# Packed attention and a two-layer MLP on one Trainium2 core: the same steps in another written order

## The chip, the core and the metric

The kernel runs on one core of a Trainium2 chip. A core has five engines that run side by side and wait for each other by semaphores: TensorE (PE in the profile; its weight loads are a row of their own, PEld), VectorE (DVE), ScalarE (ACT), GpSimd (POOL) and SyncE (SP). Matrix products go to PSUM, eight banks of 128 partitions by 512 fp32 values, and VectorE or ScalarE copy them out to SBUF. Transfers are issued from GpSimd (here the loads, which also turn fp32 into bf16) and from SyncE (here the stores and the crossbar transposes), and run on 16 DMA engines that all share. The metric is the time of one execution on the device, in microseconds (us). Each execution is timed apart; one more is taken with the hardware profiler.

## The reference

Eight batches b, eight heads, 576 positions, head size 64, and 32 packed queries p per head; then an MLP over all 4608 positions.

```python
def sm_attn(qq, kk, vv):
    s = scale * qq @ kk.T
    a = exp(s - max(s))
    return (a / (sum(a) + 1e-09)) @ vv
p_packed = sm_attn(p, k, v)              # 32 rows per head
x = sm_attn(q, p_packed, p_packed)       # 576 rows per head; heads side by side: 4608 x 512
r = maximum(x @ w_in, 0)                 # 512 -> 2048
out = (s * r * r + b) @ w_out            # 2048 -> 512, fp32
```

## The kernel before

The order of all work is written out by hand: a list of words (lines 686 to 763), run one after the other by `run` (line 638). The first engine to reach an instruction whose inputs aren't ready waits; each engine keeps its own order. A word names a step, a batch and a part; `@n` gives the PSUM banks that the step takes; a final `a` or `v` says whether ScalarE or VectorE does the step's copy; a word that comes again takes the step's next stage. The words:

- `Lk`, `Lq`, `Lv`, `Lp` load k, q, v, p of a batch (lines 124 to 153; batch 0 in parts), `Lwi6.8` loads columns 1536 to 2047 of W_in (256 per unit, line 161), `Lwo` four blocks of W_out (line 167), `Lpall` p of batches 2 to 7, `Lsb` s and b. All of these are issued by GpSimd, in the order of the words. There is one buffer each for raw k, q and v, so a load waits until the batch before has been read. GpSimd runs ahead of the words where its waits let it; it may have eight loads out.
- `PD`, `PP`, `PA`, `PPA` double p and transpose it on TensorE.
- `Tk`, `Tq` (line 222, and 248 for q of batch 0) transpose k and q of batches 0 and 1 on TensorE, with copies out of PSUM. From batch 2 on `Dk`, `Dq` (line 261) have the DMA crossbar do it: one instruction on SyncE for each, which waits for its own load and for the last reader of the destination. kT and qT have two buffers each. SyncE runs in order, so a transpose that waits also holds the stores behind it.
- `F` (line 280) is the first scores of p against k, with exp on ScalarE; `V` (line 268) reorders v on VectorE; `P` (line 305) is the packed sum over v, its reciprocal and scaling; `X` (line 332) transposes the result.
- `S` (line 339; for batch 0 in parts of 384 and 192 columns, line 366) is the second scores and exp. The sums, their ln and exp(-ln) are `A` (line 434), for batch 0 the words `d`, `l`, `i`, `G`. The weights are not applied to packed values first: `W` (line 449; 415 for batch 0) multiplies the packed values by W_in, and `M` (line 501; `h`, line 473, for batch 0) multiplies that by the attention weights, so that a hidden block of 128 rows comes out transposed, is put through relu by ScalarE or VectorE, and squared by VectorE into gT.
- `O` (line 549) does some of the 16 accumulating matmuls of a tile of 128 output rows with W_out; `Q` (line 566) scales and adds the bias while copying out on VectorE, and stores. `BT` (line 515) sums W_out for that bias.
- `Z` (line 596) is matmuls on zeros whose result nobody reads[...].

O1.4 is tile 4, counted from 0, of batch 1; A1.0 is head set 0 of batch 1; M1.8 is hidden block 8 of batch 1; a name like Q0.3 or F5.0 is read likewise. Batches overlap: while the M and O words of one batch fill TensorE, F, P, X, S, A and W of the next are spread in between. Twelve Z stand ahead of the list (line 684).

In the profile all matmuls have line 62, transposes on TensorE line 65, and all instructions of the other engines line 73, since helpers record them; groups are told apart by their tiles: kn, qn, vn are raw k, q, v, kT and qT their transposes, pw the W results, rlu the relu, ysb an output tile, banks PSUM, zb the zeros.

Of the kernel before, what the change touches and what calls it, by code (L numbers as in the profile page):

```python
# [14 lines left out]
def kernel(  # L15
# [670 lines left out]
    for word in """  # L686
        Lq0.1 PD0 PP0@1 PP0v Z4@0 Tk0.0@2 Tk0.0v Z2@0 Tk0.1@4 Tk0.1v Tk0.1v PP0a Tk0.0a F0.0@6 V0.0 F0.0
        F0.1@0 F0.1 Lp1 Z2@3 P0.0@2 P0.0 V0.1 Z3@6 X0.0 X0.0a Z1@0 P0.1 P0.1 Z3@0 X0.1 X0.1a Tq0.0@4
        Tq0.0a Z1@2 Tq0.1@3 S0.0.0@6 Tq0.1a Tq0.0v Tq0.1v S0.0.1 e0.0 e0.1 Lk1 Z1@2 S0.1.0@0 S0.1.1 e1.0
        Z1@3 d0.0@4 Lwi6.8 PD1 PP1@2 PP1v d0.1 e1.1 d1.0@6 Lwi2.4 l0.0 l0.1 d1.1 Z4@3 Tk1.1@0 l1.1 PP1v  # L690
        Tk1.1v i0.0 Tk1.0@2 Tk1.0v Tk1.0v Lwi0.1 i0.1 l1.0 i1.0 Tk1.1a Z1@6 F1.0@4 Lv1 F1.1@6 G0.1 G1.0
        Lq1 G0.0 i1.1 W0.7@0 W0.7v W0.6@2 W0.7a h0.14.0@0 h0.14.0v W0.6a W0.6a h0.12.0@2 G1.1 F1.1
        Lwi1.2 Lwi4.6 h0.14.0 Z1@6 W0.2@6 W0.2v W0.3@0 F1.0 h0.14.1@4 W0.2v h0.12.0a h0.12.0 W0.3v W0.3v
        h0.4.1@2 h0.4.1a h0.4.0@6 W0.0@2 W0.0v W0.0a h0.4.1 h0.6.1@0 h0.14.1v h0.6.1a h0.6.1 V1 h0.6.0@2
        h0.12.1@0 h0.14.1 h0.0.0@4 h0.4.0a h0.12.1a h0.4.0 h0.0.1@6 h0.0.1a h0.0.1 h0.0.0a P1.1@0 P1.1
        Z5@1 X1 h0.6.0a X1a h0.12.1 h0.0.0 Tq1.0@6 Tq1.0a Tq1.0a Tq1.1@4 W0.1@2 W1.3@0 Tq1.1v Tq1.1v
        S1@6,4 Lwo0.4 W0.1v W0.1a h0.2.0@2 W1.3v S1 W1.3v Lpall S1 h0.2.1@6 h0.2.1a A1.0@0 A1.0 W0.5@4
# [12 lines left out]
        M1.11@0 M1.11a W2.2a W2.2v O1.2x4@4 O1.0x2 O1.4x1 M1.11 M1.13 M2.14@0 M2.14a M2.15@2 O1.2x1  # L710
        O1.1x1@5 M2.15a M2.5@0 M2.15 O1.2x2 M2.5a M2.5 M2.0@2 M2.0a M2.4@0 O1.1x3 Lv3 M2.14 M2.10@2
        M2.4a PPA0 M2.10a M2.0 M1.15@0 M1.15v M1.15 O1.1x1 O1.0x1 O1.1x1 M2.6@2 O1.4x1 M2.8@0 M2.10
        M2.6v Dk4 M2.8a M2.8 O1.1x4 O1.2x1 M2.3@2 M2.3a O1.4x1 O1.2x3 O1.4x1 M2.1@0 O1.1x1 M2.3 Lk3 M2.4
        M2.1a M2.1 M2.12@2 M2.12a O1.1x2 O1.4x1 O1.2x1 O1.0x1 Dk3 O1.1x1 O1.0x3 M2.11@0 M2.11a M2.2@2
        M2.6 O1.2x1 M2.2v M2.11 O1.4x2 O1.2x1 M2.7@0 M2.7a V3 O2.0x1@2 O1.3x4@3 O1.1x1 O1.3x2 O1.0x1
        Q1.0 Lv4 O1.4x2 O1.2x1 Q1.4 O1.2x1 M2.2 Q1.2 Dq3 M2.12 M2.13@0 O1.1x1 Lq4 O2.0x4 O1.3x2 M2.13v
        O1.3x1 M2.7 O1.3x3 M2.9@6 PPA0 O1.3x4 Q1.3 M2.9a M2.9 Q1.1 O2.0x1 PPA0 M2.13 F3.0@0 F3.0 F3.1@6
        O2.0x4 F3.1 O2.0x1 O2.1x1@3 P3.1@4 P3.1 O2.0x2 V4 O2.0x3 Q2.0 X3 X3a O2.1x3 S3@0,6 S3 S3 W3.1@4
        W3.1v O2.2x1@2 W3.1v O2.2x2 A3.0@0 O2.2x1 A3.0 A3.0 A3.0 O2.1x1 A3.1@6 A3.1 A3.1 O2.2x5 Lv5
        W3.3@4 W3.3v W3.3a A3.1 W3.0@0 W3.0a W3.2@6 O2.2x5 W3.2a O2.2x1 O2.1x1 W3.2v W3.0v M3.5@4 M3.5a  # L720
        M3.10@6 M3.2@0 M3.2a M3.10v M3.5 M3.11@4 O2.2x1 M3.11a M3.1@6 M3.10 M3.12@0 M3.2 M3.1a M3.13@4
# [71 lines left out]
```

## Time and profile before

| | |
|---|---|
| median of 3 executions | 250.98 us (249.93 to 251.01) |
| the profiled execution, its own time | 249.54 us |
| its span | 247.8 us |
| busy: TensorE, VectorE, ScalarE, GpSimd | 235.5, 160.7, 125.6, 31.8 us |
| granted TensorE clock | 1.0 throughout |
| DMA, mean over the span | 143 GB/s, 35.53 MB |
| loads by GpSimd's queue | 18.58 MB |
| transposes and stores by SyncE's queue | 16.55 MB |

The span runs from the first to the last instruction of the profile, and the execution's own time holds what lies around it too. "Busy" of TensorE holds matmuls whose ends are modelled, so that 95% is not 95% of what it could do. "Waited for" lists name the engine or transfer whose semaphore came last ahead of a start. In a row of stretches, a DMA share of 1.00 is all 16 engines busy by the packets' own times; it can exceed 1, as packets overlap.

### The profile page before, as it was taken

What the parts mean: (1) busy time and instruction counts of PE and PEld (TensorE: products, weight loads), DVE (VectorE), ACT (ScalarE), POOL (GpSimd) and SP (SyncE); (2) the same over time, 40 slices, a digit from 0 to 9 for tenths busy, and PEclk for the clock granted to TensorE, in tenths of its full rate; (3) what the DMA queues carried; (4) which work ended last, traced back from release to release, by engine and by line L of the source; (5) the groups of instructions that cost most, each with busy time, mean ns of one, the idle gap of its engine ahead of it and who ended that gap; (6) DMA issues with size and microseconds to landing.
All of it is one profiled execution on the core that took longest, in us unless ns stands there. A gap on an engine that the chain in (4) does not pass through costs nothing.

```text
span 247.8 us, 5628 instructions
## 1 busy us (share of the span) xinstructions
PE 235.5 (95%) x2299; PEld 133.9 (54%) x2333; DVE 160.7 (65%) x326; ACT 125.6 (51%) x223; POOL 31.8 (13%) x45
## 2 busy tenths in 40 slices
PE   8998999998999998999999999999999999999993
PEld 2564655554556544476446645574547554675442
DVE  4438999978786477688279815983478725981232
ACT  2477798142874314865258704991288415880000
POOL 8563322001201010300110200102000000000000
PEclk9999999999999999999999999999999999999999
DMA  6999999999996889898839598998758040200135
GB/s 97 182 201 203 203 196 207 184 156 208 185 220 105 144 133 273 166 206 139 163 56 230 114 190 166 170 162 116 169 101 174 0 108 22 74 14 24 52 75 148
DMA packets 60522, 35.53 MB, mean 143 GB/s; under 512 B 32720, under 2 KB 56016, under 8 KB 60496
## 3 DMA queue, kind: packets, MB, share of 16 engines
q0 software_dynamic: 26272, 18.58, 52.8%
q1 hardware_dynamic: 34176, 16.55, 30.3%
q8 instruction: 18, 0.29, 0.5%
q14 instruction: 8, 0.07, 0.1%
q10 hardware_dynamic: 48, 0.03, 0.0%
HBM read 37.23 MB, written 9.44 MB: 188 GB/s over the span
## 4 chain that ended last, share of the span: by engine, by line
PE 82%; DVE 8%; ACT 3%; DMA 3%; issue 3%; DVEq 0%; ACTq 0%
PE banks L62 80%; DMA qT<-qn 3%; PE banks L65 2%; DVE ysb L73 2%; DVE rlu L73 2%; DVE gT L73 1%; DVE aT L73 1%; ACT rlu L73 1%; DVE pbd L73 1%; DVE kT L73 1%; ACT e L73 1%; DVE pw L73 1%; ACT rcd L73 1%; ACT pw L73 0%; ACT ld L73 0%
## 5 line engine op out<-in xcount | busy, mean ns | idle before, releaser
L62 PE MATMUL banks<-w_out_sb,gT 128*128 128x512 bf16 (+1 forms) x562 | 135.2, 373 | 2.7 <-issue 1.3
L62 PEld LDWEIGHTS <-gT 128*128 128x128 bf16 x592 | 55.9, 98 | 55.1 <-issue 4.3
L73 ACT ACTIVATE rlu<-banks 128x576 bf16<-128x576 f32 (+2 forms) x102 | 60.8, 656 | 36.1 <-PE banks L62 32.8
L62 PE MATMUL banks<-aT,pw 128*128 128x288 bf16 (+2 forms) x512 | 74.0, 286 | 2.2 <-DVE pw L73 0.9
L62 PEld LDWEIGHTS <-pw 128*128 128x128 bf16 x512 | 48.9, 98 | 25.2 <-issue 3.0
L73 DVE TENSOR_TENSOR gT<-rlu 128x576 bf16<-128x576 bf16 (+2 forms) x128 | 56.0, 455 | 9.9 <-ACT rlu L73 5.5
L73 DVE SCALAR_TENSOR_TENSOR ysb<-banks,svec,biasrep 128x512 f32<-128x512 f32 (+1 forms) x37 | 26.7, 733 | 37.5 <-PE banks L62 37.3
L73 ACT ACTIVATE e<-banks 96x768 bf16<-96x768 f32 (+3 forms) x34 | 21.8, 694 | 41.6 <-PE banks L62 41.6
L73 DVE CAST pw<-banks 128x512 bf16<-128x512 f32 (+1 forms) x40 | 23.5, 618 | 6.6 <-PE banks L62 6.6
L73 DVE TENSOR_SCALAR rlu<-banks 128x576 bf16<-128x576 f32 (+2 forms) x26 | 19.6, 761 | 6.0 <-PE banks L62 5.1
L73 POOL DMA_DIRECT2D qn<-in_q_dram x9 | 6.9, 773 | 81.1 <-DMA qT<-qn 77.5
L73 ACT CAST pw<-banks 128x512 bf16<-128x512 f32 (+1 forms) x32 | 15.8, 556 | 1.9 <-PE banks L62 1.9
L62 PE MATMUL banks<-zb 128*128 128x512 bf16 x37 | 12.7, 463 | 1.6 <-DVE zb L73 1.2
L73 DVE TENSOR_TENSOR aT<-e,rcd 128x576 bf16<-128x576 bf16 (+2 forms) x18 | 11.8, 685 | 1.6 <-ACT rcd L73 1.6
L62 PE MATMUL banks<-w_in_sb,ppd 64*32 64x512 bf16 (+1 forms) x288 | 11.2, 357 | 0.1
L73 POOL DMA_DIRECT2D kn<-in_k_dram x9 | 7.2, 805 | 29.7 <-DMA kT<-kn 23.9
L73 ACT ACTIVATE rcd<-ld 128x576 f32<-128x576 f32 (+2 forms) x18 | 10.8, 631 | 0.2
L62 PEld LDWEIGHTS <-ppd 64*32 64x32 bf16 x432 | 5.3, 89 | 10.1 <-issue 6.4
L73 ACT ACTIVATE ld<-banks 128x576 f32<-128x576 f32 (+2 forms) x18 | 10.2, 594 | 0.9 <-PE banks L62 0.4
L73 POOL DMA_DIRECT2D vn<-in_v_dram x9 | 7.0, 782 | 17.5 <-DVE vr L73 16.9
L73 DVE COPY vr<-vn 96x3072 bf16<-96x3072 bf16 (+1 forms) x9 | 7.8, 862 | 1.8 <-DMA vn<-in_v_dram 1.8
L73 DVE RECIPROCAL rd<-banks 128x2 f32<-128x2 f32 (+1 forms) x9 | 1.5, 169 | 10.6 <-PE banks L62 10.6
(54 smaller groups left out, 100.0 us busy)
## 6 DMA issues: line engine op xcount, KB each, us to landing
out_dram<-ysb SPq DMA_DIRECT2D x23, 192.0 KB, 3.4
kn<-in_k_dram POOLq DMA_DIRECT2D x7, 576.0 KB, 8.5
vn<-in_v_dram POOLq DMA_DIRECT2D x7, 576.0 KB, 9.3
qn<-in_q_dram POOLq DMA_DIRECT2D x7, 576.0 KB, 7.2
out_dram<-ysb SPq DMA_DIRECT2D x24, 128.0 KB, 2.6
w_out_sb<-in_moe_w_out_dram POOLq DMA_DIRECT2D x4, 512.0 KB, 18.1
w_in_sb<-in_moe_w_in_dram POOLq DMA_DIRECT2D x3, 512.0 KB, 11.5
out_dram<-ysb SPq DMA_DIRECT2D x23, 64.0 KB, 2.6
```

What stands on the lines that cost most here:

```text
L62: return tc.keep_in_program_order(nc.tensor.matmul(*a, **kw))
L65: return tc.keep_in_program_order(nc.tensor.transpose(*a, **kw))
L73: return lambda *a, **kw: tc.keep_in_program_order(f(*a, **kw))
```

## The change

Only the list of words changes, and with it the order of instructions on each engine. The multiset of TensorE's steps is the same but for Z: 41 matmuls on zeros before, 42 after. What moves:

- At the start, the transposes of k of batch 0 stand ahead of p's. The second scores of batch 0 are done for 192 columns first, then for 384. Four W words, not two, precede the first `h`.
- GpSimd's loads behind q of batch 0 were: p1, k1, W_in 1536-2047, 512-1023, 0-255, v1, q1, W_in 256-511, 1024-1535, W_out, pall, the rest of W_out, s and b, k2, q2, v2, q3, k4, v3, k3. They become: W_in 0-255, p1, W_in 1536-2047, 256-511, 512-1023, k1, v1, q1, W_in 1024-1535, W_out, s and b, pall, the rest of W_out, q2, k2, v2, v3, q3, k3, k4.
- `Tk1` and `F1` move from ahead of the hidden blocks of batch 0 into them.
- SyncE's order was: kT2, qT2, stores, kT4, kT3, stores, qT3, and so on. It becomes: kT2, the store of O0.3, qT2, stores of batch 0, kT3, qT3, stores, kT4, and so on. Later transposes move too.
- Some copies and relus go from ScalarE to VectorE or back: relus of `h` were 11 on ScalarE and 5 on VectorE, and are 8 and 8; those of `M` 91 and 21, now 86 and 26; copies of `W` 32 and 40, now 35 and 37.
- From the first scores of batch 5 on the two lists are the same but for a few words in another place by one or two, and bank numbers.

The diff, up to the second scores of batch 3:

```diff
     for word in """
-    Lq0.1 PD0 PP0@1 PP0v Z4@0 Tk0.0@2 Tk0.0v Z2@0 Tk0.1@4 Tk0.1v Tk0.1v PP0a Tk0.0a F0.0@6 V0.0 F0.0
-    F0.1@0 F0.1 Lp1 Z2@3 P0.0@2 P0.0 V0.1 Z3@6 X0.0 X0.0a Z1@0 P0.1 P0.1 Z3@0 X0.1 X0.1a Tq0.0@4
-    Tq0.0a Z1@2 Tq0.1@3 S0.0.0@6 Tq0.1a Tq0.0v Tq0.1v S0.0.1 e0.0 e0.1 Lk1 Z1@2 S0.1.0@0 S0.1.1 e1.0
-    Z1@3 d0.0@4 Lwi6.8 PD1 PP1@2 PP1v d0.1 e1.1 d1.0@6 Lwi2.4 l0.0 l0.1 d1.1 Z4@3 Tk1.1@0 l1.1 PP1v
-    Tk1.1v i0.0 Tk1.0@2 Tk1.0v Tk1.0v Lwi0.1 i0.1 l1.0 i1.0 Tk1.1a Z1@6 F1.0@4 Lv1 F1.1@6 G0.1 G1.0
-    Lq1 G0.0 i1.1 W0.7@0 W0.7v W0.6@2 W0.7a h0.14.0@0 h0.14.0v W0.6a W0.6a h0.12.0@2 G1.1 F1.1
-    Lwi1.2 Lwi4.6 h0.14.0 Z1@6 W0.2@6 W0.2v W0.3@0 F1.0 h0.14.1@4 W0.2v h0.12.0a h0.12.0 W0.3v W0.3v
-    h0.4.1@2 h0.4.1a h0.4.0@6 W0.0@2 W0.0v W0.0a h0.4.1 h0.6.1@0 h0.14.1v h0.6.1a h0.6.1 V1 h0.6.0@2
-    h0.12.1@0 h0.14.1 h0.0.0@4 h0.4.0a h0.12.1a h0.4.0 h0.0.1@6 h0.0.1a h0.0.1 h0.0.0a P1.1@0 P1.1
-    Z5@1 X1 h0.6.0a X1a h0.12.1 h0.0.0 Tq1.0@6 Tq1.0a Tq1.0a Tq1.1@4 W0.1@2 W1.3@0 Tq1.1v Tq1.1v
-    S1@6,4 Lwo0.4 W0.1v W0.1a h0.2.0@2 W1.3v S1 W1.3v Lpall S1 h0.2.1@6 h0.2.1a A1.0@0 A1.0 W0.5@4
-    h0.2.0v W0.5a W0.5v W0.4@6 W1.0@2 W0.4v W0.4v Lwo4.8 W1.0a W1.0v W1.1@0 W1.1a W1.1v h0.2.0
-    h0.2.1 h0.10.0@4 h0.10.0v W1.2@6 W1.2a Lwo8.12 PA W1.2a h0.8.0@2 h0.6.0 h0.8.0a h0.8.0 O0.0x1@0
-    O0.1x1@1 O0.0x2 A1.1@6 A1.1 A1.1 O0.0x1 h0.10.1@4 h0.10.1v PPA0@2,3 O0.3x4@6 A1.0 O0.2x1@7 A1.0
-    O0.2x2 A1.1 PPA0 PPA0 h0.8.1@4 O0.1x1 h0.8.1a h0.8.1 O0.3x3 O0.1x2 h0.10.0 Lwo12.16 Lsb O0.0x2
-    O0.1x2 M1.6@4 Lk2 M1.6v PPA0 O0.0x1 h0.10.1 M1.0@2 M1.0v Lq2 O0.2x1 O0.3x1 M1.8@4 M1.8v M1.8
-    O0.1x1 BT@2 M1.4@4 M1.0 O0.1x1 M1.6 M1.4a M1.4 Lv2 Dk2 O0.1x1 O0.2x1 O0.1x1 O0.3x2 O0.2x2
-    M1.10@4 M1.10a O0.1x3 O0.0x1 BT O0.1x1 M1.10 O0.1x2 V2 O0.0x1 M1.7@4 M1.7a O0.0x1 Dq2 M1.14@2
-    M1.14a O0.2x6 M1.1@4 M1.1a M1.1 M1.2@2 M1.2v M1.2 O0.2x2 O0.0x1 O0.2x1 Q0.2 O0.0x3 O0.3x1 O0.0x2
-    Q0.1 Q0.0 O0.3x3 F2.0@4 PPA0 F2.0 M1.14 F2.1@2 O1.0x1@7 M1.7 O1.0x2 M1.9@0 F2.1 P2.1@4 P2.1
-    M1.9a M1.3@2 M1.5@0 M1.3a X2 O0.3x2 M1.5a X2v W2.1@2 W2.1a M1.3 Q0.3 S2@4,0 O1.0x2 O1.4x3@6
-    W2.1v W2.0@2 S2 W2.3@4 Lq3 S2 M1.5 A2.1@0 W2.0a A2.1 O1.0x3 W2.0v M1.13@2 W2.3a W2.3v M1.12@0
-    M1.13v M1.12v M1.12 O1.4x1 A2.1 A2.1 A2.0@4 O1.4x1 M1.9 O1.4x2 Lk4 A2.0 A2.0 W2.2@2 A2.0 PPA0
-    M1.11@0 M1.11a W2.2a W2.2v O1.2x4@4 O1.0x2 O1.4x1 M1.11 M1.13 M2.14@0 M2.14a M2.15@2 O1.2x1
-    O1.1x1@5 M2.15a M2.5@0 M2.15 O1.2x2 M2.5a M2.5 M2.0@2 M2.0a M2.4@0 O1.1x3 Lv3 M2.14 M2.10@2
-    M2.4a PPA0 M2.10a M2.0 M1.15@0 M1.15v M1.15 O1.1x1 O1.0x1 O1.1x1 M2.6@2 O1.4x1 M2.8@0 M2.10
-    M2.6v Dk4 M2.8a M2.8 O1.1x4 O1.2x1 M2.3@2 M2.3a O1.4x1 O1.2x3 O1.4x1 M2.1@0 O1.1x1 M2.3 Lk3 M2.4
-    M2.1a M2.1 M2.12@2 M2.12a O1.1x2 O1.4x1 O1.2x1 O1.0x1 Dk3 O1.1x1 O1.0x3 M2.11@0 M2.11a M2.2@2
-    M2.6 O1.2x1 M2.2v M2.11 O1.4x2 O1.2x1 M2.7@0 M2.7a V3 O2.0x1@2 O1.3x4@3 O1.1x1 O1.3x2 O1.0x1
-    Q1.0 Lv4 O1.4x2 O1.2x1 Q1.4 O1.2x1 M2.2 Q1.2 Dq3 M2.12 M2.13@0 O1.1x1 Lq4 O2.0x4 O1.3x2 M2.13v
-    O1.3x1 M2.7 O1.3x3 M2.9@6 PPA0 O1.3x4 Q1.3 M2.9a M2.9 Q1.1 O2.0x1 PPA0 M2.13 F3.0@0 F3.0 F3.1@6
-    O2.0x4 F3.1 O2.0x1 O2.1x1@3 P3.1@4 P3.1 O2.0x2 V4 O2.0x3 Q2.0 X3 X3a O2.1x3 S3@0,6 S3 S3 W3.1@4
-    W3.1v O2.2x1@2 W3.1v O2.2x2 A3.0@0 O2.2x1 A3.0 A3.0 A3.0 O2.1x1 A3.1@6 A3.1 A3.1 O2.2x5 Lv5
...
+    Tk0.0@2 Lq0.1 Tk0.0v Tk0.0v PD0 Z2@0 PP0@1 PP0v Tk0.1@4 PP0v Tk0.1a Tk0.1v F0.0@6 F0.0 F0.1@2
+    F0.1 V0.0 Z2@1 P0.0@0 P0.0 V0.1 Z3@6 X0.0 X0.0v Z1@2 P0.1 P0.1 Z3@2 X0.1 Tq0.0@4 Tq0.0v Tq0.0v
+    Z1@2 Tq0.1@1 S0.0.0@6 Tq0.1v Z1@4 S0.1.0@2 Lwi0.1 X0.1v Tq0.1a S0.1.1 e1.1 W0.0@4 e1.0 Z1@0
+    d1.1@0 l1.1 Lp1 d1.0 S0.0.1 l1.0 Lwi6.8 PD1 PP1@2 PP1v e0.0 Z2@3 d0.0@0 PP1v e0.1 d0.1 Z3@6
+    W0.6@2 W0.0v W0.0v W0.6v i1.1 W0.7@6 i1.0 l0.1 i0.1 G0.1 Lwi1.2 l0.0 Z4@4 W0.1@4 i0.0 G0.0 W0.6a
+    W0.1a W0.1a G1.1 Z1@0 h0.12.0@0 W0.7a W0.7a h0.0.0@2 h0.0.0a Lwi2.4 G1.0 h0.14.1@4 h0.12.0v
+    h0.12.0 Z1@6 W0.2@6 W0.2a Lk1 W0.2a h0.14.1v Lv1 h0.2.0@0 h0.14.1 h0.14.0@2 h0.14.0a Lq1 h0.0.0
+    h0.2.0v h0.2.0 h0.4.1@4 h0.4.1v h0.14.0 W0.3@6 W0.3v W0.3a Lwi4.6 h0.4.0@0 h0.4.0a Tk1.0@2
+    Tk1.0v Tk1.0v Tk1.1@4 Tk1.1v Tk1.1a h0.0.1@6 F1.0@0 h0.0.1a F1.0 F1.1@2 h0.4.0 h0.4.1 h0.0.1
+    h0.6.0@4 h0.2.1@6 V1 F1.1 h0.12.1@0 P1.1@2 P1.1 Z4@3 X1 h0.6.0a h0.2.1a h0.2.1 h0.12.1v h0.12.1
+    Lwo0.4 h0.6.1@4 Lsb Tq1.1@6 X1a h0.6.1v Tq1.1a Tq1.1a Tq1.0@2 Tq1.0v W1.0@0 h0.6.1 Tq1.0v W1.0v
+    W1.0v S1@4,6 S1 S1 Z1@2 W0.4@2 W0.4v Lpall Lwo4.8 W0.5@4 W0.5a W0.5v W0.4v Lwo8.12 W1.1@0 A1.0@6
+    W1.1a h0.10.0@4 W1.1v A1.0 h0.10.1@2 h0.10.1a A1.1@0 A1.1 A1.1 h0.10.0v h0.8.1@6 h0.10.1 A1.0
+    Lwo12.16 W1.3@2 W1.2@4 O0.3x1@0 h0.8.1v O0.3x1 O0.1x1@1 W1.3a W1.3v O0.2x3@6 h0.8.1 O0.3x2 A1.1
+    O0.1x1 h0.8.0@2 O0.1x2 W1.2a W1.2a h0.8.0a h0.10.0 h0.6.0 A1.0 M1.0@4 M1.0a PA O0.2x1 h0.8.0
+    O0.1x1 M1.3@2 M1.6@4 M1.6v O0.3x2 M1.6 M1.3a Lq2 M1.3 O0.2x1 M1.14@2 M1.14a M1.5@4 O0.3x1 M1.5v
+    M1.5 O0.2x1 PPA0@7,2 M1.9@4 PPA0 O0.1x3 M1.9a M1.9 BT@3 M1.4@4 PPA0 O0.3x3 O0.2x1 M1.4a O0.0x2@7
+    O0.3x3 Lk2 O0.3x1 O0.0x5 O0.3x2 M1.1@4 O0.2x2 BT O0.0x1 O0.2x1 M1.10@2 M1.4 M1.0 O0.0x1 O0.2x1
+    O0.0x3 M1.1a M1.1 Lv2 M1.15@4 Dk2 Q0.3 O0.1x4 O0.0x1 M1.10v O0.0x2 M1.14 O0.2x2 O0.1x1 M1.10 V2
+    O0.2x1 Dq2 O0.0x1 O1.0x1@0 M1.15v M1.15 O0.2x2 F2.0@2 F2.0 F2.1@4 F2.1 O0.1x2 Q0.0 O0.1x1 Q0.2
+    M1.2@6 P2.1@2 M1.2a Q0.1 M1.12@4 M1.12a M1.8@6 P2.1 M1.2 X2 O1.0x3 M1.8v M1.8 X2a W2.2@4 W2.2v
+    W2.2v S2@2,6 S2 S2 O1.4x2@1 O1.0x2 M1.11@2 Lv3 A2.0@4 A2.0 A2.0 O1.4x3 M1.7@6 M1.7a M1.11v
+    O1.3x1@2 M1.11 A2.1@4 A2.0 O1.4x1 O1.3x2 Lq3 PPA0 M1.13@6 M1.13v O1.3x1 O1.1x3@3 M1.12 A2.1
+    W2.1@4 W2.1a W2.1v M1.7 W2.0@6 O1.1x1 O1.0x1 O1.4x1 O1.1x2 A2.1 W2.0a W2.0a O1.1x1 M1.13 O1.1x2
+    A2.1 O1.1x2 Lk3 Dk3 M2.0@4 M2.0a O1.0x1 M2.10@6 M2.10a M2.10 O1.4x1 O1.1x2 W2.3@4 M2.2@6 M2.2v
+    Dq3 O1.1x2 M2.2 O1.3x3 O1.0x1 W2.3v O1.0x1 W2.3a M2.8@6 M2.8v M2.8 O1.0x2 M2.5@4 M2.5a M2.5
+    O1.1x1 O1.0x1 M2.6@6 M2.7@4 M2.7a M2.6v M2.6 Q1.1 V3 O1.4x1 O1.0x1 M2.0 O1.4x5 M2.1@6 O1.4x1
+    M2.1a M2.3@4 M2.3a M2.7 O1.2x1@3 M2.4@6 O1.4x1 Q1.4 M2.4a M2.4 O1.2x2 M2.13@4 O1.3x2 M2.15@6
+    O1.2x1 M2.1 M2.13a O2.0x1@1 M2.13 Lk4 O1.3x1 O1.2x1 PPA0 M2.15a M2.11@4 O1.3x2 M2.11a M2.11
+    O1.0x1 O1.3x3 M2.3 M2.9@6 M2.12@4 M2.12v M2.12 O1.2x1 O1.0x1 O1.2x1 Q1.0 Lv4 O1.2x3 M2.14@4
+    M2.9a O1.3x1 PPA0 PPA0 PPA0 O1.2x1 O2.0x3 M2.9 Lq4 M2.14v O1.2x1 M2.15 O1.2x1 Dk4 PPA0 O1.2x1
+    Q1.3 O1.2x2 O2.0x1 M2.14 O2.0x1 Q1.2 Dq4 F3.0@6 F3.0 F3.1@4 O2.0x3 O2.2x1@0 F3.1 O2.0x2 P3.1@2
+    P3.1 O2.0x5 X3 X3v O2.2x3 S3@6,4 W3.2@2 Q2.0 W3.2v O2.2x2 S3 O2.1x1@1 A3.0@6 O2.1x1 S3 A3.1@4
+    W3.2v O2.2x1 A3.0 O2.2x1 A3.1 A3.1 V4 O2.2x1 W3.3@2 W3.3v A3.0 W3.0@6 W3.0a W3.0a W3.1@4 O2.1x2
...
```

## The prediction

> **What bounds the kernel now.** I read the page's head first, then who waited for whom on TensorE, then busy time by stretch, then the DMA queues.
>
> From the page:
>
> ```profile
> span 247.8 us, 5628 instructions
> PE 235.5 (95%) x2299; PEld 133.9 (54%) x2333; DVE 160.7 (65%) x326; ACT 125.6 (51%) x223; POOL 31.8 (13%) x45
> PE 82%; DVE 8%; ACT 3%; DMA 3%; issue 3%; DVEq 0%; ACTq 0%
> L62 PE MATMUL banks<-zb 128*128 128x512 bf16 x37 | 12.7, 463 | 1.6 <-DVE zb L73 1.2
> ```
>
> TensorE is busy 95% of the span, the chain is 82% TensorE, and some of that is idle matmuls on zeros (the words Z; 41 in the program, 37 recorded). The change leaves every useful matmul in place, so it can only move waits and Z's. Since a matmul's end is modelled, I cost work by pitch: in the order of time, 13 matmuls of 128x512 take 2.97 us from 55.34, so (2.97-0.38)/12 = 0.216 each; 16 of 128x288 take 2.12 from 105.19, so (2.12-0.286)/15 = 0.122. Likewise for the other kinds. Summing pitches along the word list against the start of each word's weight loads gives the time lost: 4.35 us by the first hidden block (21.3), 5.0 by the first output matmul (36.95), 6.15 at the first scores of batch 2 (58.2), 7.25 at its second scores (63.9), 8.1 at batch 4 (121.7), 7.55 at the first scores of batch 5 (148.6). From there both orders are the same words with few exceptions, and the multiset of TensorE words ahead of that point is the same but for one Z. So the whole difference is: one Z, plus after's loss minus before's at F5.0.
>
> The recorded waits on TensorE, over the span:
>
> ```profile
> PE banks L62 <- DVE ysb L73: 1.1, 2, 0.5
> PE banks L62 <- DMA qT<-qn: 1.0, 1, 1.0
> PE banks L62 <- DVE pw L73: 0.9, 3, 0.4
> ```
>
> The first is 59.66 and 60.97 (banks held by outputs not yet evicted), the second is S3, the second scores of batch 3, at 99.55. A good order can win no more than these and some hidden ones.
>
> Stretches from 20 us (columns: PE, weight loads, DVE, ACT, POOL busy; clock; DMA share; GB/s):
>
> ```profile
> 25.00:30.00 5.00, 4.67 (x86) 2.92 (x84) 4.46 (x13) 3.80 (x8) 1.58 (x2) 1.00 1.34 201
> 30.00:35.00 5.00, 4.90 (x94) 2.85 (x93) 4.60 (x12) 4.67 (x10) 1.69 (x3) 1.00 1.30 204
> 35.00:40.00 5.00, 4.95 (x60) 2.78 (x53) 5.00 (x12) 4.60 (x9) 2.03 (x3) 1.00 1.50 197
> ```
>
> Here VectorE is full, ScalarE nearly, and loads run at 200 GB/s without a gap: this stage has no slack on any engine. Then the first crossbar transpose (issued at 49.92, 8.3 us to landing) meets the loads of q and v of batch 2:
>
> ```profile
> 49.00:52.00 3.00, 2.95 (x17) 1.57 (x17) 2.90 (x5) 0.65 (x1) 0.00 (x0) 1.00 1.32 204
> 53.00:54.00 1.00, 1.00 (x7) 0.50 (x6) 0.97 (x3) 0.91 (x2) 0.00 (x0) 1.00 0.75 86
> 54.00:55.00 1.00, 1.00 (x9) 0.64 (x8) 0.46 (x1) 0.00 (x0) 0.00 (x0) 1.00 0.94 81
> 56.00:57.00 1.00, 1.00 (x6) 0.48 (x5) 0.74 (x1) 0.00 (x0) 0.00 (x0) 1.00 1.20 266
> ```
>
> Mixed, the traffic falls from 204 to about 85 GB/s; alone, transposes move 225 to 266. TensorE hardly waits for it here.
>
> [...]
>
> **Part 1, to the first hidden block.** W_in columns 0 to 255 come right behind q of batch 0 and most of W_in ahead of k1, v1, q1. Landings of before give the rates (288 KB 1.5 us, 576 KB 2.9, 512 KB 2.5, 256 KB 1.4; q0 complete at 13.98). So after: W_in 0-255 at 15.4, 1536-2047 at 18.1, 256-511 at 19.5, 512-1023 at 22.0, k1 24.9, v1 27.8, q1 30.7, 1024-1535 33.2, W_out complete at 47 as before. First uses, walked as below: 15.95, 18.85, 20.5, 22.95, 26.05, 29.1, 32.1, 34.7: slack of 0.55 to 1.5 us, no wait, but a late load is seen one for one. k0's transposes now come ahead of p0's: k0's second half (7.92) is still awaited and the first scores end at 9.6 instead of 9.69: -0.1. Then the scores of part 1 (96 columns) go first and four W blocks, not two, precede the first hidden block; it waits for ACT's chain of exp, ln, exp and for Z3 and Z4. First hidden block at about 21.0, loss 5.0 instead of 4.35: +0.65.
>
> **Part 2, to the first output matmul.** k1's transposes move from 17.9, when VectorE was 2.79 of 5 us busy, into the hidden blocks. VectorE's queue from 21.8, by pitches (0.87 a relu of 768, 0.47 a square of 768 or relu of 384, 0.27 a square of 384, 0.33 a 256-column copy, 0.38 a kT copy): 0.87+0.47+0.47+0.27+0.47+0.87+0.47+0.47+0.47+0.33 = 5.16, and three kT copies 1.2: kT1 complete at 28.15. TensorE is there at 27.4, does 0.2 of it and stands: 0.58. Again S1 wants qT1, whose last copy ends at 34.07 behind six other VectorE operations, 0.55. Before lost 0.7 in this stage (S1 there too), after 1.05: +0.35. Behind the late k1 copies stand the squares of three hidden blocks, v1's reordering, then P1.1; Z4 covers that.
>
> **Part 3, to S2.** Before loses 2.25: about 0.6 at 45 (M1.8 and its neighbour take 1.32 for 0.70 of pitch), 0.3 ahead of F2.0, 1.1 for the two outputs, rest small. After evicts Q0.3 early and has Q0.0 and Q0.2 ahead of M1.2, so the 1.1 goes; I find M1.0 waiting 0.25 for A1.0 and 0.5 in all: -1.5, after the bias sums that both have. F2.0 stands at 59.4. Its transpose starts when k2 lands (second of the three loads now, 52.8); v2 (landing 56.2) is still out, since the instruction waits for its own load alone. At 8.3 us as before it lands at 61.1; if it flows from 56.2 at 225 GB/s (2.6 us) at 59. I take 59.4: no wait.
>
> **Part 4, S2.** qT2's transpose is on SP behind kT2's and two stores (0.9): issue about 58.4, and 4.5 to 4.9 us alone: 63.1; S2 is at 64.3. But v3's load is now first in GpSimd's queue, waiting only for V2 (VectorE, about 58.35), where before q3 was first and waited for qT2 itself. They collide. The nearest row is the transpose of 157.00 with a load issued at 157.55: 10.0 us to landing. So the wait is 0 to 4.1; I take +0.4. What waits behind: all TensorE.
>
> **Part 5.** S3's wait goes, since q3's transpose now follows k3's directly, at about 75, not at 93: -0.7 of loss. One more Z: +0.22. In the rest (transposes of 4 to 7, each tens of us early) SP and GpSimd cost nothing: TensorE never waits for them in this trace either; without that cover a late transpose would cost its lateness.
>
> Sum: 0.65+0.35-1.5+0.4-0.7+0.2 = -0.6 us. Span 247.8 to 247.2, profiled execution 249.54 to 248.9. The runs' median, 250.98, lies 1.4 above that execution, so 250.4.
>
> **Rivals.** (B) Faster: my VectorE walk is pessimistic (pitches overlap more, or Z3 and Z4 hide the queue) and S2 doesn't wait: parts 1, 2 and 4 shrink to 0.2, giving -1.8: 249.2, down to 248.5. For it: before, with VectorE 5.00 of 5 at 35 to 40, lost nothing there. Against: the queue sum is plain. (C) Slower: qT2 lands at 66.5 to 68.4 because of v3, S2 waits 2.2 to 4.1 instead of 0.4: 252.2 to 254.1. It decides once qT2 lands more than 1.9 us later than I took, at 66.6. For it the row of 10.0; against, qT2 may flow before v3's packets do. (D) The change doesn't do what it says, as kT2 still starts under v2: lands at 61.1, F2.0 waits 1.7, S2 moves with it: about 251.7; or a W_in or k1 load is a microsecond late: 251.4 to 253.
>
> **How the numbers follow.** Mine 0.45 (own range 249.7 to 251.6), B 0.28, C 0.17, D 0.10. A change under 0.5% (1.25 us) can hardly be told from none here: faster below 249.7, slower above 252.2. B is mostly faster, C and half of D slower: 0.29, 0.47, 0.24. The range leaves out the ends of B and C: 248.6 to 253.2.
>
> **What would show it.** Right: the wait at S3 and the two for ysb gone; waits for DVE kT or qT near 28 and 34; first output matmul near 38.4, F2.0 near 59.4, F5.0 near 148. Part 4 wrong: a wait for DMA qT at 64 above a microsecond. Part 1 wrong: waits for DMA w_in or kn ahead of 35. Wrong as a whole if F5.0 is moved by waits after 100 us that I haven't seen.

## The result, and the profile after

| | before | after |
|---|---|---|
| median, taken side by side (20 executions each) | 250.91 us | 250.52 us |
| lowest and highest | 249.33, 253.12 | 249.38, 251.46 |
| the profiled execution, its own time | 249.54 | 250.76 |
| its span | 247.8 | 249.0 |

The ratio is 0.9982, with an interval of 0.9962 to 1.0002: no difference that this measurement can tell from none. Two lines of the table go opposite ways, and most of what follows is about that: the medians say 0.4 us faster, the two profiled executions say 1.2 us slower. (Ratios, here and below, leave out executions more than 1.5% above the fastest of the same kernel; medians and extremes keep them.)

The head of the page of after, then the chain's shares, answering the lines shown of before:

```profile
span 249.0 us, 5653 instructions
...
PE 238.4 (96%) x2334; PEld 133.7 (54%) x2334; DVE 165.7 (67%) x336; ACT 121.5 (49%) x213; POOL 30.6 (12%) x45
...
PE 77%; DVE 9%; DMA 6%; ACT 4%; issue 2%; POOL 0%; SPq 0%; POOLq 0%; ACTq 0%; DVEq 0%
```

The chain's share of transfers has doubled, from 3 to 6%: q's transpose has 3% of it in both, and what came in is the load of k of batch 0 at the start, with 2%. Who TensorE waited for, over the span:

```profile
PE banks L62 <- DMA qT<-qn: 1.2, 1, 1.2
...
PE banks L62 <- DVE ysb L73: 0.5, 1, 0.5
PE banks L62 <- ACT rlu L73: 0.5, 1, 0.5
```

The first line reads almost like before's (1.0 for one wait), but it is another wait. S3 no longer stands. The wait is now S2's, at 66 us. What SyncE issued there (start, time to issue, what):

```profile
52.47 2.97 SPq L73 DMA_TRANSPOSE kT<-kn  x1
58.01 0.81 SPq L73 DMA_DIRECT2D out_dram<-ysb  x2
58.94 3.00 SPq L73 DMA_TRANSPOSE qT<-qn  x1
62.09 3.72 SPq L73 DMA_DIRECT2D out_dram<-ysb  x6
```

And GpSimd:

```profile
60.54 0.77 POOL L73 DMA_DIRECT2D vn<-in_v_dram  x1 [21.77 <-DVE vr L73]
67.99 0.77 POOL L73 DMA_DIRECT2D qn<-in_q_dram  x1 [6.68 <-DMA qT<-qn]
```

SyncE was free at 55.44 and q2 had landed at 49.45, yet qT2's transpose went out at 58.94: the stores of O0.3 stood ahead of it and waited for their eviction. 1.6 us later v3's load joined in, and qT2 landed at 67.41, 8.5 us after its issue. So there are two suspects for the wait, one a place in SyncE's order and one a place in GpSimd's; the experiments take them one at a time.

The early stretches of after:

```profile
25.00:30.00 5.00, 4.33 (x72) 3.20 (x70) 4.97 (x13) 3.54 (x6) 1.51 (x2) 1.00 1.32 204
30.00:35.00 5.00, 4.74 (x103) 3.22 (x101) 4.11 (x11) 3.53 (x7) 0.74 (x2) 1.00 1.26 208
35.00:40.00 5.00, 4.72 (x74) 2.58 (x74) 4.84 (x11) 4.21 (x9) 2.32 (x3) 1.00 1.51 185
```

The second figure is TensorE's. It was 4.67, 4.90 and 4.95 before, so 0.16 to 0.34 us more of each stretch is idle. VectorE is at 4.97 and 4.84 of 5 in the first and last.

### The profile page after: what moved, and what is told of

It reads as the page before. It is cut to its first block, busy times and chain, and to the rows that moved or that the text cites. A ratio compares the mean times of both kernels' runs of the same rounds, so it can differ in the third digit from the quotient of the medians.

```text
span 249.0 us, 5653 instructions
## 1 busy us (share of the span) xinstructions
PE 238.4 (96%) x2334; PEld 133.7 (54%) x2334; DVE 165.7 (67%) x336; ACT 121.5 (49%) x213; POOL 30.6 (12%) x45
## 4 chain that ended last, share of the span: by engine, by line
PE 77%; DVE 9%; DMA 6%; ACT 4%; issue 2%; POOL 0%; SPq 0%; POOLq 0%; ACTq 0%; DVEq 0%
PE banks L62 76%; DMA qT<-qn 3%; DMA kn<-in_k_dram 2%; DVE gT L73 2%; DVE rlu L73 2%; ACT rlu L73 1%; DVE bias L73 1%; ACT e L73 1%; DVE qT L73 1%; DVE pbd L73 1%; DVE biasrep L73 1%; PE banks L65 1%; ACT rcd L73 1%; DVE ysb L73 1%; ACT ld L73 0%
## 5 line engine op out<-in xcount | busy, mean ns | idle before, releaser
L62 PE MATMUL banks<-w_out_sb,gT 128*128 128x512 bf16 (+1 forms) x592 | 140.9, 374 | 0.0
L73 ACT ACTIVATE rlu<-banks 128x576 bf16<-128x576 f32 (+2 forms) x94 | 57.7, 656 | 33.3 <-PE banks L62 19.8
L73 DVE TENSOR_TENSOR gT<-rlu 128x576 bf16<-128x576 bf16 (+2 forms) x128 | 55.3, 454 | 12.8 <-ACT rlu L73 9.6
L73 DVE TENSOR_SCALAR rlu<-banks 128x576 bf16<-128x576 f32 (+2 forms) x34 | 25.1, 741 | 6.7 <-PE banks L62 2.7
L73 DVE CAST pw<-banks 128x512 bf16<-128x512 f32 (+1 forms) x37 | 22.3, 634 | 5.1 <-PE banks L62 5.0
L73 ACT CAST pw<-banks 128x512 bf16<-128x512 f32 (+1 forms) x35 | 16.4, 538 | 1.9 <-PE banks L62 1.9
L62 PE MATMUL banks<-zb 128*128 128x512 bf16 x42 | 13.8, 440 | 1.2 <-DVE zb L73 1.2
L73 POOL DMA_DIRECT2D vn<-in_v_dram x9 | 6.7, 748 | 38.4 <-DVE vr L73 37.1
L62 PEld LDWEIGHTS <-kT 128*128 128x128 bf16 x192 | 6.8, 98 | 2.6 <-ACT kT L73 0.5
```

What stands on the lines that cost most here:

```text
L62: return tc.keep_in_program_order(nc.tensor.matmul(*a, **kw))
L73: return lambda *a, **kw: tc.keep_in_program_order(f(*a, **kw))
```

## The experiments

Times in us. "In place" means the loss by pitches, worked out as in the prediction. The rows were taken in three comparisons, each with its own executions of the kernel before ("before beside it"), so medians of different comparisons are not to be read to a tenth: the third row has a lower median than the fourth and a higher ratio.

| | median | lowest to highest | before beside it | ratio |
|---|---|---|---|---|
| changed, q2's transpose ahead of the stores | 249.72 | 249.34 to 251.88 | 251.0 | 0.9963 (0.9940 to 0.9986) |
| changed, v3's load behind q3's and k3's | 249.58 | 249.12 to 250.28 | 251.0 | 0.9960 (0.9944 to 0.9977) |
| before, q3's transpose early | 248.61 | 248.28 to 249.89 | 251.0 | 0.9931 (0.9905 to 0.9956) |
| changed, q2 ahead and A1.0 ahead | 249.02 | 248.61 to 250.52 | 251.0 | 0.9914 (0.9889 to 0.9939) |
| old start, new rest | 249.91 | 248.70 to 251.50 | 250.82 | 0.9973 (0.9949 to 0.9997) |
| new start, old rest | 250.88 | 249.58 to 256.48 | 250.82 | 0.9994 (0.9963 to 1.0024) |
| before, six Z ahead of S3 | 250.19 | 249.49 to 255.58 | 250.21 | 0.9994 (0.9966 to 1.0022) |
| before, q3 early, O0.0 out first | 248.71 | 247.67 to 252.19 | 250.21 | 0.9942 (0.9913 to 0.9970) |
| changed, VectorE's queue shorter | 248.77 | 248.42 to 249.79 | 250.21 | 0.9952 (0.9930 to 0.9973) |
| changed, all moves | 248.83 | 248.29 to 250.91 | 250.21 | 0.9946 (0.9920 to 0.9971) |

### Why S2 stands: two ways to remove it

```diff
-M1.15@4 Dk2 Q0.3 O0.1x4 O0.0x1
+M1.15@4 Dk2 Dq2 Q0.3 O0.1x4 O0.0x1
...
-O0.2x1 Dq2 O0.0x1 O1.0x1@0
+O0.2x1 O0.0x1 O1.0x1@0
```

> The changed order with one word moved: the transpose of q2 stands directly behind that of k2 on SyncE, ahead of the two stores of O0.3. Theory (late issue plus collision): in the changed kernel SyncE stands until 58.01 us at the stores of O0.3, so qT2 is issued at 58.94 and lands at 67.41 with v3's load beside it, and S2 stands some 1.5 us. Moved, it is issued at about 55.5, once k2's is off SyncE, lands between 60 and 61, and the wait for it at S2 is gone: 250.5 becomes about 249.0. Rival 1: S2 is held anyway, by the W copy or the relu behind it: 250.5. Rival 2: kT2 itself now lands later, as the two transposes share the queue, and F2.0 at 60.5 waits: 250.5 to 252.

SyncE of this kernel:

```profile
52.80 2.97 SPq L73 DMA_TRANSPOSE kT<-kn  x1
55.90 2.99 SPq L73 DMA_TRANSPOSE qT<-qn  x1
```

Issued at 55.90, qT2 landed at 60.42, 4.5 us later, and the wait is gone from TensorE's list. kT2 took 5.1 us from its issue to its landing at 57.89, against 5.0 without the move, so the second transpose did not slow the first. The other way:

```diff
-M1.11@2 Lv3 A2.0@4
+M1.11@2 A2.0@4
...
-O1.1x2 Lk3 Dk3
+O1.1x2 Lk3 Lv3 Dk3
```

> The changed order with one word moved: v3's load behind those of q3 and k3 in GpSimd's order, so it starts only once qT2 has landed; qT2 is still issued late, at about 58.9 us. Theory (the collision with v3's load): qT2 lands 4.5 to 5 us after its issue, at about 63.7, instead of 8.5 us after; the wait for it at S2 (66 us) is gone: about 249.0. Rival: it is the five stores behind it, or the transpose of k2 just before, that make it slow: it still lands after 66.5 and the time stays at 250.5.

Here qT2 was still issued late, at 59.10, with the same stores behind it, but no load beside it:

```profile
L73 SPq DMA_TRANSPOSE qT<-qn x1: 2911/2911/2911, 59.1 to 59.1; - x1
...
DMA to landing us min/median/max: 4.4/4.4/4.4
```

4.4 us instead of 8.5, and no wait. So the load of v3 is what doubled it; the stores and the transpose of k2 are cleared. In place either move takes 1.4 us out of S2. The medians are 0.8 and 0.9 below the changed kernel's 250.52, which was taken in another comparison; by the ratios to before (0.9982, and now 0.9963 and 0.9960) it is about 0.5 us. Why the times fell by less than the 1.4 that left S2 is not shown. The first 20 us vary by themselves: the same start lost 4.57 to 5.74 us up to the first hidden block in seven profiles (the highest two with waits of 0.9 and 1.0 us for k and W_in, though a third profile with such a wait lost less).

### What S3 was worth

```diff
-Dk3 O1.1x1 O1.0x3
+Dk3 Dq3 O1.1x1 O1.0x3
...
-Q1.4 O1.2x1 M2.2 Q1.2 Dq3 M2.12
+Q1.4 O1.2x1 M2.2 Q1.2 M2.12
```

> The kernel before with one word moved: the transpose of q3 directly behind that of k3 on SyncE, ahead of the stores of batch 1. It does alone what my fifth part says the change does for S3. Theory: the wait of 0.95 us for qT3 at S3 (99.55 us) is gone and nothing takes its place: 250.9 becomes about 250.0 (ratio 0.996). Rival: S3 is held next by the sum P3.1, the turned values X3 or by banks, and the time stays within 0.3 us of before.

One word moved in the kernel before, and its median fell from 251.0 to 248.6; the wait at S3 was gone, and in place 1.0 us with it, as its profile had promised. But 2.4 us went from the median. Even by the ratio (0.69% of 251.0) it is 1.7. So the kernel before as a rule loses more by this word than the execution that I had read. Two further profiles of it show one way.

> The kernel before, unchanged, profiled once more. The profiled execution that I predicted from took 249.54 us, 1.4 below the median of its runs, and moving q3's transpose alone (e3_before_q3_early) won 2.4 us where that profile had a wait of 0.95 us to win. Theory: qT3's landing differs from execution to execution, since its transpose is issued beside the loads of v4 and q4; in an execution near the median of 250.9 the wait for it at S3 is 2 us or more, and all else in the trace is as before. Rival: the wait at S3 is again about 1 us, and the other 1.4 us lie somewhere else.

> As b1_before_again, a third profile of the kernel before. If the theory holds, the times of the three executions differ by as much as their waits at S3 do, to within 0.3 us.

They took 252.31 and 252.22 us. TensorE around S3 in the first of them:

```profile
97.61 0.81 PE L62 MATMUL banks<-w_out_sb,gT 128*128 128x512 bf16 x3
100.69 0.44 PE L62 MATMUL banks<-qT,ppd 64*32 64x288 bf16 x16 [2.28 <-DMA qT<-qn]
```

and by stretches (the columns are those of the prediction; the clock is the third figure from the end):

```profile
100.00:101.00 1.00, 0.31 (x24) 0.25 (x23) 0.00 (x0) 0.00 (x0) 0.00 (x0) 1.00 0.35 92
101.00:102.00 1.00, 1.00 (x23) 0.37 (x5) 0.53 (x1) 0.92 (x2) 0.79 (x2) 1.00 0.85 264
102.00:103.00 1.00, 1.00 (x5) 0.49 (x4) 0.77 (x2) 0.71 (x2) 1.00 (x2) 0.52 0.75 185
103.00:104.00 1.00, 1.00 (x4) 0.46 (x3) 0.05 (x1) 0.97 (x3) 0.49 (x1) 0.50 0.92 58
104.00:105.00 1.00, 1.00 (x4) 0.38 (x3) 0.71 (x1) 0.97 (x2) 0.00 (x0) 0.50 1.00 137
105.00:106.00 1.00, 1.00 (x19) 0.27 (x25) 0.00 (x0) 0.25 (x1) 0.00 (x0) 0.77 1.31 187
```

qT3 landed at 100.65 instead of 99.51, TensorE stood 2.28 us, and then the granted clock was half: the shares missing from 1.00 add up to 0.48 + 0.50 + 0.50 + 0.23 = 1.71 us, which is 3.42 us at half clock. The second of them stood longer still, and lost the same 1.71 (clocks of 0.57, 0.50, 0.50 and 0.72 in four stretches):

```profile
PE banks L62 <- DMA qT<-qn: 2.4, 1, 2.4
```

In the first profile of before the stand was 0.95 and the clock stayed at 1.00. From S3 to hidden block M3.1 the loss grew by 0.25 us in that first profile and by 3.25 and 3.34 in these two, which is all of the 2.7 us between their times and somewhat more.

Why qT3 came later is open. Its transpose was issued at the same time in all three profiles (93.08, 93.09 and 92.95), and v4's load landed at 93.83, 94.10 and 94.03; q4's load, which I had named too, was issued only afterwards. Yet the transpose took 6.4, 7.6 and 7.7 us.

How often does an execution lose time this way? Each one has its mean granted clock on record, for 138 of the 158 executions of the kernel before. Losing 1.71 of 250 us gives a mean clock of 0.993, which is what the two further profiles have, and 42 of the 138 have 0.993 or less. They took 251.84 to 254.46 us (median 253.0). The other 96 have a median of 250.4, and only three of them are above 251.75. So the two further profiles show the slower third. The first profile, at 249.54, is near the lowest of all, 249.3. An ordinary execution at full clock has no trace.

In the comparison of this experiment 24 of 62 executions of the kernel before have such a clock, and 1 of the 12 with the word moved, which lost next to nothing by it (248.75 us). At full clock the median goes from 250.46 to 248.58, so the word is worth 1.9 us there: the 0.95 of the first profile, and about as much again that separates that profile from a median execution. With the word moved this distance is gone (the profiled execution took 248.63), so it goes with the place of that word; where in the trace it lies isn't shown. The rest of the 2.4 is the executions whose clock fell. Of the changed kernel's 20, 1 has 0.993 (251.28 us).

Does the stand itself bring the clock down? Six matmuls on zeros in the place of the stand:

```diff
-X3a O2.1x3 S3@0,6
+X3a O2.1x3 Z6@0 S3@0,6
```

> The kernel before with six more matmuls on zeros directly ahead of S3, where TensorE stands for qT3; nothing else moves. In the two further profiles of the kernel before TensorE stood 2.3 to 2.4 us there and the granted clock then fell to 0.50 for some 3 us, which lost another 1.8 us; in the first profile it stood 0.95 us and the clock stayed. Theory (a long stand lowers the clock): six matmuls are 1.3 us at full clock, so at most about 1.1 us of standing is left and the clock stays; an execution of the first kind costs 0.3 us more (249.9), one of the other 1.8 less (250.4), so the median falls from 250.9 to about 250.1 and the slowest executions come below 251.5. Rival (the clock falls for another cause): the median is 250.9 or more, and executions of 253 stay.

In its profiled execution (250.23 us) qT3 landed at 100.13, nearly as late as above, and TensorE had this:

```profile
98.24 0.81 PE L62 MATMUL banks<-w_out_sb,gT 128*128 128x512 bf16 x3
98.88 1.46 PE L62 MATMUL banks<-zb 128*128 128x512 bf16 x6
100.27 0.44 PE L62 MATMUL banks<-qT,ppd 64*32 64x288 bf16 x16
```

No stand, and a clock of 1.00 in each stretch from 96 to 106 us. But this doesn't test the theory: without the six matmuls the stand here would have been 1.2 us (from 99.05 to 100.27), no longer than stands elsewhere that were not followed by half clock. The median is that of before beside it, and 2 of 14 executions had clocks of 0.991 and 0.990 and took 254.8 and 255.6; of before beside it 5 of 33 had 0.993 or less. So the six matmuls did not remove the falls of the clock; I have no trace of those executions. What ties the clock to the stand is the three stands of 1.86 us or more (the third is in the next section) that were each followed by half clock, where shorter ones were not, and the clocks of the executions: 24 of 62 of before at 0.993 or less, against 4 of 75 of the four kernels beside it in which S3 no longer waits. S3 is not the only place for it, as two kernels of the section on the changed start show (7 and 6 of 22).

### M1.0 and the bank waits

To the first experiment's kernel:

```diff
-h0.8.0a h0.10.0 h0.6.0 A1.0 M1.0@4
+h0.8.0a A1.0 h0.10.0 h0.6.0 M1.0@4
```

> As e1_q2_ahead_of_store, and on VectorE the last step of the weights A1.0 ahead of the squares of two hidden blocks (h0.10.0 and h0.6.0), where the changed order has it behind them. In the changed kernel M1.0 stands some 0.8 us for these weights at 42 us; my prediction had 0.25. Theory: the two squares are 0.94 us of VectorE's queue, so M1.0's wait is gone and the time is 0.8 us below e1's, about 248.2, since qT2 no longer is a fixed point behind it. Rival: the squares, now later, hold the output matmuls that read them, or the first transposes set F2.0 and S2 at a fixed time, and the time is e1's within 0.2 us.

TensorE at M1.0, in the changed kernel and in this one:

```profile
43.02 0.66 PE L62 MATMUL banks<-aT,pw 128*128 128x288 bf16 x4 [0.46 <-ACT rlu L73]
...
42.61 0.65 PE L62 MATMUL banks<-aT,pw 128*128 128x288 bf16 x4
```

249.72 became 249.02, 0.7 us; M1.0's wait is gone and nothing replaced it. Then the two waits for evictions, each with one swap on VectorE:

```diff
-O0.0x2 Q0.1 Q0.0 O0.3x3
+O0.0x2 Q0.0 Q0.1 O0.3x3
```

> As e3_before_q3_early (248.6), and the eviction of output tile O0.0 ahead of that of O0.1 on VectorE, since a hidden block (M1.9) takes O0.0's bank at 60 us and stands about 0.9 us for it. It asks what the two waits for ysb in the kernel before were worth, which my third part put at 1.1 us. Theory: one eviction is 0.66 us of VectorE's queue, so 0.6 us go: 248.0. Rival: S2 is held next by qT2 (landing 61) or by VectorE's next operations and the time stays within 0.2 us of 248.6.

It stayed at 248.7, and the swap in the changed kernel (with the moves of the next section) did as little:

```diff
-O0.1x2 Q0.0 O0.1x1 Q0.2 M1.2@6
+O0.1x2 Q0.2 O0.1x1 Q0.0 M1.2@6
```

> As e9_new_vector_queue_shorter, and the eviction of O0.2 ahead of that of O0.0 on VectorE, since M1.2 takes O0.2's bank and stands about 0.9 us for it at 62 us. Theory: one eviction of 0.66 us less in front of it, 0.5 to 0.6 us less than e9: about 247.8, the fastest of all. Rival: F2.0 at 60 us now comes up against kT2's landing (58.3), or S2 against its other inputs, and the time is e9's.

The trace of the latter says why:

```profile
62.32 0.28 PE L62 MATMUL banks<-aT,pw 128*128 128x288 bf16 x1
62.98 0.53 PE L62 MATMUL banks<-aT,pw 128*128 128x288 bf16 x3 [0.38 <-DVE ysb L73]
```

A hidden block takes two banks (`take(2)` in `mlp_in`): M1.2 needs banks 6 and 7, so both O0.2's and O0.0's eviction, whichever is first. One of its matmuls starts earlier, and the second stands. M1.9 takes banks 0 and 1 likewise.

The profiled execution of the swap in the kernel before took 252.19 us, and shows what q3's early transpose can bring on. TensorE stood at the first matmul of O2.2:

```profile
101.15 0.92 PE L62 MATMUL banks<-w_out_sb,gT 128*128 128x512 bf16 x2 [1.86 <-DVE ysb L73]
```

The eviction that it waited for itself waited for an output buffer, of which there are five, until a store landed at 100.22. That store had been issued at 91.67, behind qT3's transpose, which landed only at 98.59, with v4's load beside it. After the stand of 1.86 us the clock was half again (0.64, 0.50, 0.50 and 0.65 in the four stretches from 101 us), for the same 1.71 us of loss. The word that cures S3 thus puts the stores at risk. In the two kernels that have it with the old start, 1 of 20 executions was above 250 us; behind the changed start (the mirror in the next section) 8 of 22 were above 251.75, and whether this is the cause there isn't known.

### What the changed start costs

> The start of the kernel before, up to its first output matmul, and behind it what the changed order has, with the two moves of e4_q2_ahead_and_a1_ahead; no computation is left out, Z's are those of before. It asks what the changed start costs. My prediction had 1.0 us for it; the traces have the first output matmul at 36.95 against 39.35 us and the loss there at about 5.2 against 6.8 to 7.0. Theory (the trace's figure): 1.6 to 2.0 us less loss there, one Z (0.2) less, but kT2, whose landing near 58 us the load of k2 sets, now holds F2.0 by 0.3 to 1: e4's 249.0 becomes 247.2 to 248.0. Rival 1 (my prediction's figure): 248.0 to 248.3. Rival 2: the loads set the pace up to F2.0, so that an earlier start wins nothing: 249.0.

The edit is the join itself: the old list up to `O0.0x1@0`, then of the new list what is not done yet, with the moves of the kernel above. At 249.9 it missed every expectation, and it says nothing on the start: between S1 and the first output matmul it lost 1.8 us, where before loses 0.2, and 7 of its 22 executions have a clock of 0.992 or 0.993. The new rest there has h, A and O steps spaced for a start that still had W blocks between them, which may be why. The mirror joins better:

> The mirror of it: the changed start, up to its first output matmul, and behind it the rest of the kernel before with q3's transpose early, as in e3_before_q3_early (248.6). Theory: the start costs 1.6 to 2.0 us, and one Z 0.2: 250.4 to 250.8. By my prediction's figure, 1.0 and the Z: 249.8. Rival: later waits (for banks at 59 to 61 us) take up the delay: 248.6 to 249.2.

Its profiled execution took 249.76 us against 248.63 with the old start. In place the start costs 1.8 us by F2.0 (loss of 8.22 against 6.39), and only 0.85 by S2, since the old rest's waits for banks at 59 to 61 us are then partly over before TensorE comes. The price of the start is thus 1.8 us where it falls, and 1.1 at the end, one Z included. The median, 250.9, contains 8 of 22 executions above 251.75 for which I have no trace: five with a clock of 0.993 or less, and three at full clock (252.4 to 253.2), so that the clock is not all of it. They stay open.

```diff
-W0.3@6 W0.3v W0.3a Lwi4.6
+W0.3@6 W0.3a W0.3a Lwi4.6
...
-Tq1.1@6 X1a h0.6.1v Tq1.1a Tq1.1a
+Tq1.1@6 X1a h0.6.1a Tq1.1a Tq1.1a
...
-Tq1.0@2 Tq1.0v W1.0@0 h0.6.1 Tq1.0v W1.0v
+Tq1.0@2 Tq1.0v W1.0@0 Tq1.0v h0.6.1 W1.0v
```

> As e4_q2_ahead_and_a1_ahead (249.0), and three operations taken out of VectorE's queue ahead of the last copies of kT1 and qT1: one copy of W0.3 and the relu of h0.6.1 go to ScalarE, and the square of h0.6.1 stands behind the last copy of qT1. In the changed kernel F1.0 stands about 0.5 us and S1 about 1.0 us. Theory (my second part: these waits are VectorE's queue): F1.0 starts about 0.3 us and S1 0.3 to 0.6 us earlier, 248.2 to 248.5. Rival: ScalarE's own queue (its copies of kT1 and qT1) holds the same points, and the time stays within 0.2 us of 249.0.

248.77 against 249.02, taken in different comparisons: too close to tell. The traces say that nothing was won in this stage. In the kernel with q2 and A1.0 ahead, S1 stood:

```profile
32.74 0.27 PE L65 MATMUL banks<-identb,pk 128*128 128x128 bf16 x2
...
35.36 0.43 PE L62 MATMUL banks<-qT,ppd 64*32 64x288 bf16 x14 [0.34 <-DVE qT L73]
```

and with the shorter queue X1 stands instead:

```profile
32.52 0.27 PE L65 MATMUL banks<-identb,pk 128*128 128x128 bf16 x2 [0.46 <-DVE pk L73]
...
34.50 0.80 PE L62 MATMUL banks<-qT,ppd 64*32 64x288 bf16 x16
```

F1.0 began 0.3 us earlier, as VectorE's walk said; from the first hidden block to M1.0 the loss was 2.06 us, against 1.93 without the moves. What was gained at F1.0 was lost again behind it. My reading is that a chain of short steps over several engines (exp on ScalarE, packed sum on TensorE, reciprocal, scaling and copies) bounds this stage; one trial suggests it and doesn't show it.

Five of these kernels beat both originals: the kernel before with q3's transpose early, without and with O0.0 out first, and the changed one with q2 and A1.0 ahead, alone, with the shorter queue and with all moves. They are at 248.6 to 249.0, where before beside them is at 250.2 and 251.0. The differences between the five are too small to rank them.

## Why the prediction was right, and where it wasn't

250.4 was forecast and 250.5 measured, but errors of nearly 2 us cancel in it: the hit is in good part luck. Point by point, as loss in the profiled executions, after minus before:

| step | forecast | traces |
|---|---|---|
| part 1, to the first hidden block | +0.65 | +0.50 |
| part 2, to the first output matmul | +0.35 | +1.43 |
| part 3, from there to S2 | -1.5 | -0.85 |
| part 4, S2 to A2.0 | +0.4 | +1.65 |
| part 5, A2.0 to F5.0 (S3's wait) | -0.7 | -1.67 |
| one Z | +0.2 | +0.2 |
| sum | -0.6 | +1.26 |

The sum of the traces is the 1.2 us by which the spans differ. (Each loss carries the 0.5 us or so by which one start differs from the next. The profile of before is near the fastest of its executions and that of after is not, so the last row compares two draws and not the two kernels.)

**Part 1** held: the first hidden block stood at 20.88 where I had 21.0. Three loads landed about 1.2 us later than forecast (k1 at 26.08, q1 at 31.95, W_in 1024-1535 at 34.46), without a wait for one of them. **Part 2** had the right places (F1.0 and S1, for kT and qT copies) and half the size (1.05 us of loss in the changed kernel forecast, about 2.1 in its trace): kT1 was complete at 28.95, not 28.15, and qT1 at 35.08, not 34.07, the first output matmul at 39.35, not 38.4. The walk added VectorE's operations one behind the other and took their inputs as ready; X1's and P1.1's turns between the engines were left out. That it is VectorE's queue alone is not what the runs showed: shortening it moved the wait to X1. **Part 3** mis-sized two terms: M1.0 stood 0.8 us for its weights behind two squares, where I had 0.25 (shown by moving them), and the wait for evictions did not go but came to M1.2, which needs both banks.

**Part 4** is the step that failed outright. Its pieces were there: the issue (58.4 forecast, 58.94), v3's load behind it, the row of 10.0 us. I took 0.4 from a range of 0 to 4.1, on the hope that qT2 would flow before v3's packets; that was rival C's mechanism against my own, and C was right: 67.41 lies in its 66.5 to 68.4. Its price of 252.2 to 254.1 was not: TensorE came to S2 at 66 and not at 64.3, so the wait was 1.2 us, not 2.2 to 4.1. The place cost 1.2 to 1.4 us in the profiles, and about 0.5 by the ratios.

**The last step**, "The runs' median, 250.98, lies 1.4 above that execution, so 250.4", is what saved the number, for a reason that it didn't know. It carries the 1.4 over as if it belonged to the measurement. But a good part of it goes with the place of q3's transpose: with that one word moved, the median at full clock lies on the profiled execution. The change moves this transpose too, so it had no such 1.4 to carry, and its median lies 0.24 below its profiled execution. What it gained lies, as far as 20 executions show it, in the falls of the clock: 1 of 20 has 0.993 or less, against 42 of 138 of before (5 of 33 in the comparison with the fewest). At full clock the two kernels can't be told apart, with medians of 250.4 and 250.5 from different comparisons. Of **part 5**, the mechanism was right and the size was not: 1.9 us at full clock, by the medians 2.4, not 0.7. (In the table's -1.67, which has the first profile of before, S3's wait is 0.95; the other 0.7 is spread over the stage and I can't name it.) That gain paid for parts 2 and 4.

The fall "from 204 to about 85 GB/s" is read from chosen rows: transpose and load were both out from 49.92 on, and the traffic was still 204 to 52 and 212 in the next us; only 53 to 55 had 81 to 86. What v3's load cost q2's transpose is read from the landings: 4.4 us from its issue at 59.10 without that load beside it, 8.5 us from 58.94 with it.

Rival B is out, as S2 and S1 stood. Rival D's late loads and its wait at F2.0 did not come: kT2 landed 5.0 us after its issue at 57.51, ahead of F2.0, though v2's load was still out until 55.28, for 2.8 of the 5.0 us. The runs don't settle how long a load must flow beside a transpose to slow it: qT2 of after took 8.5 us with v3's load out from 1.6 us after its issue to its end, but qT3 of before took 6.4 to 7.7 us with v4's load out for its first 0.8 to 1.1 us alone.

## What to carry to other kernels

Issue a crossbar transpose as soon as its input has landed, ahead of stores that wait for an eviction on the same queue (q2's went out at 55.90 instead of 58.94), and order the next load behind its landing (4.4 us to landing instead of 8.5); but look what stores then stand behind it, and whether their buffers last (one issued behind q3's early transpose at 91.67 landed at 100.22, and TensorE stood 1.86 us). A wait read in one profile is one draw: where lowest, median and profiled time lie apart, compare the mean granted clocks of all executions and take another profile, before the difference is carried over as an offset. A wait can cost twice: in three traces a stand of TensorE of 1.9 to 2.4 us was followed by 1.7 us lost to a lower clock.

## What the runs showed of the hardware

Stands of TensorE of 1.86 us (q3 early with O0.0 out first), 2.28 and 2.4 us (the two further profiles of before) were each followed by about 3.4 us at a granted clock of 0.50, 1.71 us of loss every time, beginning 0.1 to 1.4 us after matmuls had started again. Stands of 0.95 (before), 1.2 (changed) and 1.3 us (old start, new rest) were not: the clock is 1.00 in the stretches from 98 to 108 us of before and from 66 to 72 of the changed kernel, and 1.0 is the mean of the whole execution of the third. That is three traces of each kind, and the rows around the 1.86 us have thin work too (TensorE was busy 1.12 us of the three from 98 to 101), so whether the length of a stand decides it, where between 1.3 and 1.9 us, and whether thin work counts, isn't shown.
